# First keys and values of an attention kernel: VectorE halves two rows of each third, GpSimd adds one, and six rows are turned ahead of three

## The chip, the cores and the metric

One core of one Trainium2 chip runs the whole program. The metric is the device time of one execution in microseconds (us), inputs in the chip's memory (HBM) at the start and the output there at the end. The engines named below are TensorE (PE in the profile; PEld is its loading of weights), VectorE (DVE), ScalarE (ACT), GpSimd (POOL) and SyncE (SP), which issues most of the DMAs. Each engine runs its own queue in order and waits for the others through semaphores.

## The reference

Two parts, the second fed by the first (q and k are drawn with 0.8 times unit normal values, v with 0.1):

```python
# q, k, v: (8, 8, 576, 64); pool = 8, so Sp = 72
k_p = k.reshape(B, H, Sp, pool, D).mean(axis=3)
v_p = v.reshape(B, H, Sp, pool, D).mean(axis=3)
scores = scale * np.matmul(q, k_p.transpose(0, 1, 3, 2))
scores = scores - np.max(scores, axis=-1, keepdims=True)
attn = np.exp(scores)
attn = attn / (np.sum(attn, axis=-1, keepdims=True) + 1e-09)
attn_out = np.matmul(attn, v_p)
# x = attn_out as 4608 rows of 512; 8 experts, capacity 1152
logits = x @ w_gate
expert_idx = np.argmax(logits, axis=1)
...
h = np.maximum(np.einsum('ecd,edf->ecf', disp, w1), 0.0)   # F = 1024
y = np.einsum('ecf,efd->ecd', h, w2)
out[i] = gate_w[i] * y[expert_idx[i], pos[i]]              # rows kept by the capacity
```

The change lies in the first two lines (mean over 8 consecutive rows of k and v) and in what stands directly behind them.

## The kernel before

The function `pooled_attn_top1_moe` emits its instructions under one manual schedule: the order in which Python emits them is the order on each engine's queue. Nothing is reordered afterwards; only semaphores decide when an instruction starts.

**Pooled keys and values.** Batches go in pairs. K and V of a pair come as three thirds each, a third being a raw tile of 128 partitions x 3 rows x 512 floats (8 rows of 64 that are to be added), loaded by SP (L207) in the order k, k, k, v, v, v, with q tiles between (L223, tails L228). Seven raw buffers exist. GpSimd adds a third by halves in `tree`: 512 to 256 for each row (L370), to 128 (L372), to 64 (L374, into kp or vp). So it goes for the later pairs. For the first pair the work is split: GpSimd adds four of the nine rows (the first third and one row of the last), VectorE the other five with a reduction over the pool axis (`red`, L380).

**Turning.** TensorE transposes the pooled rows, two rows in one 128x128 transpose and the ninth alone (`turns_of`, L399 and L401), into PSUM. Copies (L406, L412) lay them out: keys into `kbs`, values into `vTp`. For the first pair ScalarE copies the even rows of batch 0, VectorE the odd and the ninth. `prep_v` then multiplies the values of a batch by the block with the expert gates (L463, TensorE) and VectorE masks the product into `vbd` (L470, L471).

**Units.** Attention is cut into 36 units of 128 query rows: four full tiles for each of two batches and one tail for both, 9 to a pair. The main loop's step n holds: the scores of unit n (L499) in two halves, its row maximum (L506) and subtraction (L511) on VectorE, the exponential of unit n-1 on ScalarE (L514), the transposes of the probabilities of unit n-2 in two parts (`p_t`: L523 on TensorE, L524 on ScalarE), the transposes of the next unit's q (L489) with ScalarE's copy qT (L490), the product with the values of unit n-2 (`av`, L535), its division (L546 to L554), and steps of the routing. Finished rows are written to `xs` from ScalarE's queue (L582). `load_kv(1)` stands ahead of the loop, `load_kv(2)` at step 5; GpSimd's trees for pair 1 are queued from step 0.

**Shared completion semaphores.** The loads of SP and the writes of xs take turns over a set of eight completion semaphores (DMAHW0 to DMAHW7 in the listings), so a DMA also waits for the one that had its semaphore last.

Behind the attention come the routing's end and the experts (from about 210 us to the end), which the change leaves as they are.

Of the kernel before, what the change touches and what calls it, by code (L numbers as in the profile page):

```python
# [21 lines left out]
P = 128  # L22
# [9 lines left out]
def pooled_attn_top1_moe(ctx: ExitStack, tc: tile.TileContext, q, k, v, wg, w1, w2, cap, out):  # L32
# [135 lines left out]
    with ExitStack() as actx:  # L168
# [207 lines left out]
                left[due] -= 1  # L376
            yield

        def red(dst, t):
            nc.vector.tensor_reduce(out=dst, in_=t.rearrange("p c (j d) -> p c d j", j=POOL), axis=AX.X, op=ALU.add)  # L380

        def pooled(p):

# [3 lines left out]
        def third(i):  # L387
            return slice(i * NR // 3, (i + 1) * NR // 3)
# [41 lines left out]
            summed("v", p)  # L430
            copies(vTp, slice(0, None), turns_of(bank([P, 4, P], "pk"), vps[p]))

        def keys_first(u, made):

            if u:
                for x in range(2):
                    copies(kbs[0][x * D : (x + 1) * D, x, u], slice(u * H + x, (u + 1) * H, 2), made)
                return
            for o, copy in ((0, nc.scalar.copy), (1, nc.vector.tensor_copy)):
                for x in range(2):  # L440
                    v, hs = kbs[0][x * D : (x + 1) * D, x, 0], slice(x, H, 2)
                    done = [even(v, hs, made, o, copy)]
                    if o:
                        done.append(last(v, hs, made, copy))
                    for d_ in done:
                        if o == 0:
                            tc.add_to_no_dep_group("first", d_.ins)
                        else:
                            tc.declare_no_dep(d_.ins, group="first", reason="other columns, other quadrants")

        def values_first(u, made):
            if u == 0:
                last(vTp, slice(0, None), made)
            for o in range(2):
                even(vTp[:, u * H : (u + 1) * H], slice(u * H, (u + 1) * H), made, o)

        def prep_v(b):

# [16 lines left out]
        class Unit:  # L475
# [16 lines left out]
            def score(self, part):  # L492
                if part == 0:
                    self.ps = psc.tile([P, HH, 256], F32, name="ps", tag="ps")
                m = P // len(self.bs)
                for h in range(part * HH // 2, (part + 1) * HH // 2):
                    for u, b in enumerate(self.bs):
                        us = slice(u * m, (u + 1) * m)
                        nc.tensor.matmul(self.ps[us, h, 0 : 2 * SP_].rearrange("p (a x) -> p a x", a=2), self.qT[:, h, us],  # L499
                                         kbs[b // 2 % 2][:, :, b % 2, h], start=True, stop=True)  # L500

            def softmax(self):

# [260 lines left out]
        with tc.manual_schedule():  # L764
            rest = setup()
            pooled(0)
            head_masks()
            gq.append(tree(kps[0][:, third(0)], raws[0][0][0]))
            gq.append(tree(kps[0][:, NR - 1 :], raws[0][0][2][:, 2:3]))
            gq.append(tree(vps[0][:, third(0)], raws[0][1][0]))  # L770
            gq.append(tree(vps[0][:, 6:7], raws[0][1][2][:, 0:1]))
            drain(gq)
            red(kps[0][:, third(1)], raws[0][0][1])
            red(kps[0][:, 6 : NR - 1], raws[0][0][2][:, 0:2])
            load_kv(1)
            pk = psc.tile([P, HH, 256], F32, name="ps", tag="ps").rearrange("p a n -> p (a n)")[:, 0:512].rearrange("p (i q) -> p i q", i=4)
            kfirst = turns_of(pk, kps[0])
            keys_first(0, kfirst)
            units[0].q_part()
            gates_in()  # L780
            red(vps[0][:, third(1)], raws[0][1][1])
            red(vps[0][:, 7:], raws[0][1][2][:, 1:])
            vfirst = []

            def ahead(b):

# [312 lines left out]
            def turns(n):  # L1099

                p, j = divmod(n, NPU)
                if n == 1:
                    prep_v(0)
                    values_first(1, vfirst[0])
                if p + 1 < B // 2:
                    if j == (6 if p == 0 else 5):
                        prep_k(p + 1)
                    if j == (8 if p == 0 else 6):
                        turn_v(p + 1)
# [10 lines left out]
            def spread(n):  # L1120

                p, j = divmod(n, NPU)
                if n == 1:
                    vfirst.append(turns_of(bank([P, 4, P], "pk"), vps[0]))
                    values_first(0, vfirst[0])
                elif values_at(n):
                    prep_v(values_at(n))

# [19 lines left out]
            for n in range(nu + 2):  # L1148
# [21 lines left out]
                    start_rows()  # L1170
                if u:
                    u.score(0)
                if p and n <= nu:
                    p.p_t(0)
                if 0 < n <= nu:
                    units[n - 1].exp()
                fed = n > NB and nx and values_at(n)
                if fed:
                    nx.q_part()
                spread(n)  # L1180
                if u:
                    u.score(1)
                    if n == 0:
                        keys_first(1, kfirst)
                    u.softmax()
                step(aq)
                if p and n <= nu:
                    p.p_t(1)
                if n == nu:
                    sums()  # L1190
                if nx and not fed:
                    nx.q_part()
                if held:
                    held.clear()
                    step(rq)
# [173 lines left out]
```

## Time and profile before

| what | us |
|---|---|
| three runs | 663.55, 661.72, 657.91 |
| median | 661.72 |
| profiled execution, its own time | 656.15 |
| span of the profiled execution | 654.5 |
| TensorE busy in the span | 607.1 (93%) |
| VectorE / GpSimd / ScalarE busy | 339.2 / 317.9 / 223.6 |
| mean granted TensorE clock | 0.979 of full speed |

How to read it: the span runs from the first to the last recorded instruction of one execution, and 1.65 us lie around it. All times in the rows are counted from the span's start. A row of the timeline gives start, duration, engine, line, operation, output <- inputs, shapes and count; in brackets stands how long the engine had been idle before it and what ended that.

### The profile page before, as it was taken

The numbers are of one execution on the slowest core, as the hardware profiler recorded it, in microseconds if no ns is written. First come the engines' busy times: TensorE is split into PE (matmuls) and PEld (weight loads), VectorE is DVE, ScalarE is ACT, GpSimd is POOL, SyncE is SP. The second block draws the span as 40 slices with busy tenths as digits, with TensorE's granted clock in tenths as the row PEclk, the third lists the DMA queues.
The fourth block names the chain that finished last, engine by engine and source line by source line (L and its number), as shares of the span: only waits on it lengthen the run. The fifth ranks groups of instructions, "written<-read, shape, count | busy, mean of one in ns | idle before, by whom it ended". The sixth has DMA issues, their size and how long they took to land. (4 is left out here: it accounts for less than half of the span.)

```text
span 654.5 us, 13915 instructions
## 1 busy us (share of the span) xinstructions
PE 607.1 (93%) x3966; PEld 539.8 (82%) x3967; DVE 339.2 (52%) x740; ACT 223.6 (34%) x414; POOL 317.9 (49%) x537
## 2 busy tenths in 40 slices
PE   2899979989779799999999999999999999999994
PEld 2789869878668588898989899888998889989983
DVE  4777867868767812246728642235432565222222
ACT  2465444546424111135517521115211473112111
POOL 7399979247645334215745413414444155431344
PEclk9999989999979899999999999999999999999997
DMA  9999996584622271107845652102721091110111
GB/s 314 301 255 334 310 264 121 118 242 98 177 46 54 73 300 64 32 32 238 298 159 178 248 204 64 64 20 77 263 64 56 12 316 31 64 42 22 64 48 65
DMA packets 103712, 93.79 MB, mean 143 GB/s; under 512 B 82820, under 2 KB 82820, under 8 KB 103688
## 3 DMA queue, kind: packets, MB, share of 16 engines
q1 hardware_dynamic: 54520, 62.47, 30.1%
q0 software_dynamic: 11392, 21.57, 10.4%
q10 hardware_dynamic: 37776, 9.46, 6.5%
q8 instruction: 12, 0.20, 0.1%
q14 instruction: 12, 0.10, 0.1%
HBM read 132.96 MB, written 31.27 MB: 251 GB/s over the span
## 5 line engine op out<-in xcount | busy, mean ns | idle before, releaser
L1269 DVE SCALAR_TENSOR_TENSOR hl<-ph,hh 128x512 fp32r<-128x512 f32 x60 | 40.8, 690 | 108.9 <-ACT hh L1268 78.0
L1268 ACT ACTIVATE hh<-ph 128x512 fp32r<-128x512 f32 x60 | 35.9, 599 | 171.2 <-PE ph L152 168.3
L165 PE MATMUL y<-w2h,hh 128*128 128x512 f32 x280 | 78.1, 400 | 0.0
L152 PE MATMUL ph<-xh,w1h 128*128 128x256 f32 x480 | 76.5, 281 | 1.2 <-ACT xo L1084 0.9
L165 PE MATMUL y<-w2l,hh 128*128 128x512 f32 x280 | 76.6, 395 | 0.0
L152 PE MATMUL ph<-xl,w1h 128*128 128x256 f32 x480 | 76.2, 280 | 0.4 <-DVE w1l L128 0.3
L152 PE MATMUL ph<-xh,w1l 128*128 128x256 f32 x480 | 76.0, 280 | 0.0
L97 POOL DMA_INDIRECT xg<-xs,ix x42 | 44.2, 1053 | 58.9 <-PE y L165 52.2
L165 PE MATMUL y<-w2h,hl 128*128 128x512 f32 x280 | 71.0, 396 | 0.0
L152 PEld LDWEIGHTS ph<-xh,w1h 128*128 128x128 f32 x480 | 65.7, 188 | 4.5 <-issue 1.9
L152 PEld LDWEIGHTS ph<-xl,w1h 128*128 128x128 f32 x480 | 65.0, 188 | 0.7 <-issue 0.7
L152 PEld LDWEIGHTS ph<-xh,w1l 128*128 128x128 f32 x480 | 65.0, 188 | 0.0
L165 PEld LDWEIGHTS y<-w2h,hl 128*128 128x128 f32 x280 | 52.6, 188 | 12.7
L165 PEld LDWEIGHTS y<-w2l,hh 128*128 128x128 f32 x280 | 52.6, 188 | 12.6
L535 PE MATMUL pa<-vbd,pT 126*128 126x146 f32 (+5 forms) x400 | 60.6, 313 | 0.0
L535 PEld LDWEIGHTS pa<-vbd,pT 126*128 126x128 f32 (+1 forms) x400 | 56.4, 184 | 3.0 <-issue 0.7
L165 PEld LDWEIGHTS y<-w2h,hh 128*128 128x128 f32 x280 | 50.0, 188 | 9.4
L524 ACT COPY pT<-pp 126x384 f32<-126x384 f32 x72 | 30.3, 422 | 78.6 <-PE pp L523 56.7
L128 DVE TENSOR_TENSOR xl<-px,xh 128x512 fp32r<-128x512 f32 x40 | 25.7, 686 | 57.2 <-ACT xh L127 57.2
L102 POOL DMA_INDIRECT out_dram<-zrow,iz x40 | 46.8, 1171 | 16.3 <-issue 15.1
L499 PE MATMUL ps<-kbs,qT 128*128 128x144 f32 (+1 forms) x320 | 52.9, 308 | 1.8 <-ACT qT L490 1.8
L95 POOL TENSOR_TENSOR guard<-ix 128x4 int32<-128x4 int32 x21 | 5.1, 244 | 101.6 <-DVE ix L92 101.3
(261 smaller groups left out, 1035.6 us busy)
## 6 DMA issues: line engine op xcount, KB each, us to landing
r<-in_moe_w_dram SPq DMA_DIRECT2D x86, 1024.0 KB
raw<-in_k_dram SPq DMA_DIRECT2D x12, 768.0 KB
raw<-in_v_dram SPq DMA_DIRECT2D x12, 768.0 KB
qblk<-in_q_dram SPq DMA_DIRECT2D x32, 256.0 KB
xs<-xo ACTq DMA_DIRECT2D x16, 512.0 KB
raw<-in_moe_w_dram SPq DMA_DIRECT2D x4, 512.0 KB
qtail<-in_q_dram SPq DMA_DIRECT2D x8, 128.0 KB
xs<-xo ACTq DMA_DIRECT2D x8, 128.0 KB
```

The costliest lines, as they stand in the source:

```text
L95: nc.gpsimd.tensor_sub(guard, ix, ix)
L97: nc.gpsimd.indirect_dma_start(out=dst[:, i, :].bitcast(F32), out_offset=None, in_=src, in_offset=bass.IndirectOffsetOnAxis(ap=ix[:, i, 0: ...
L102: ins = nc.gpsimd.indirect_dma_start(out=out[:, :], out_offset=bass.IndirectOffsetOnAxis(ap=i_, axis=0), in_=src, in_offset=None, bounds_c ...
L128: eng.tensor_sub(lo, src, hi.bitcast(F32))
L152: nc.tensor.matmul(p[:, f2], a[:, c, f * P : (f + 1) * P], b[:, c], start=(f2 == 0 and j == 0 and c == 0), stop=(f2 == 1 and j == 2 and c ...
L165: nc.tensor.matmul(y, a[:, c, i * P : (i + 1) * P], b[:, c], start=(first and n == 0), stop=(last and n == len(terms) - 1))
L499: nc.tensor.matmul(self.ps[us, h, 0 : 2 * SP_].rearrange("p (a x) -> p a x", a=2), self.qT[:, h, us], kbs[b // 2 % 2][:, :, b % 2, h], sta ...
L524: nc.scalar.copy(self.pT[:, cs.start : cs.stop], pp[0:KC, 0 : len(cs)])
L535: made = nc.tensor.matmul(self.pa[us, h0 * XW : (h0 + nh) * XW], self.pT[:, c, us], vbd[b % 2][:, c, 0:nh].rearrange("r s x -> r (s x)"), ...
L1268: nc.scalar.activation(hh[s], p, AF.Relu)
L1269: nc.vector.scalar_tensor_tensor(out=hl[s], in0=p, scalar=0.0, in1=hh[s].bitcast(F32), op0=ALU.max, op1=ALU.subtract)
```

## The change

- `red` goes. `pair_sum` takes its place on VectorE: rows 0 and 1 of a third are added by three halving adds (128x512, 128x256, 128x128 results), with scratch from the pool of the `xo` tiles. VectorE so takes six of nine rows, GpSimd the last row of each third, K's three first and then V's.
- K: six rows (three transposes, `turn_six`) are turned as soon as the first two thirds are pooled, then q of unit 0, then the last three rows (`turn_three`, two transposes). ScalarE lays out the six, VectorE and ScalarE the three.
- q of unit 1 is turned between the two halves of unit 0's scores; the keys of batch 1 are laid out behind that (`keys_one`), by ScalarE (six rows, row 8) and VectorE (rows 6 and 7).
- V: VectorE's three sums stand behind those copies, with the softmax of unit 0 between the first and the second. The six rows are turned in step 1, then the first part of unit 0's probabilities, q of unit 2, and the three rows. `prep_v(0)` moves from the end of step 1 to between the halves of unit 2's scores.

```diff
@@ -376,8 +376,14 @@

-        def red(dst, t):
-            nc.vector.tensor_reduce(out=dst, in_=t.rearrange("p c (j d) -> p c d j", j=POOL), axis=AX.X, op=ALU.add)
+        def pair_sum(dst, t):
+            sc = wk.tile([P, 2, H, XW - 1], F32, name="xo", tag="xo", bufs=3).rearrange("p i h x -> p (i h x)")
+            t1 = sc[:, 0:W].rearrange("p (i x) -> p i x", i=2)
+            t2 = sc[:, W : 3 * W // 2].rearrange("p (i x) -> p i x", i=2)
+            nc.vector.tensor_add(t1, t[:, :, 0 : W // 2], t[:, :, W // 2 :])
+            nc.vector.tensor_add(t2, t1[:, :, 0 : W // 4], t1[:, :, W // 4 :])
+            nc.vector.tensor_add(dst, t2[:, :, 0:D], t2[:, :, D:])

@@ -430,29 +436,45 @@

-        def keys_first(u, made):
...
-        def values_first(u, made):
...
+        turned = pall[:, 0 : 3 * P].rearrange("p (i q) -> p i q", i=3)
+        def turn_six(x):
+            for i in range(3):
+                nc.tensor.transpose(turned[:, i], x[:, 2 * i : 2 * i + 2].rearrange("p r d -> p (r d)"), ident)
+        def turn_three(x):
+            aside(nc.tensor.transpose(side[0:D, 0:P], x[:, 6], ident))
+            aside(nc.tensor.transpose(side[:, P : 2 * P], x[:, 7:9].rearrange("p r d -> p (r d)"), ident))
+        def laid(v, hs, src, rs, copy=nc.scalar.copy):
+            return copy(v.rearrange("d h (g r) -> d h g r", r=NR)[:, :, :, rs], src.rearrange("d i (h g) -> d h g i", g=GP)[:, hs])
+        def six(v, hs):
             for o in range(2):
-                even(vTp[:, u * H : (u + 1) * H], slice(u * H, (u + 1) * H), made, o)
+                laid(v, hs, turned[o * D : (o + 1) * D], slice(o, 6, 2))
+        def three(v, hs, copy=nc.scalar.copy):
+            made = [laid(v, hs, side[D:, P : 2 * P].rearrange("d (i q) -> d i q", i=1), slice(8, 9)),
+                    laid(v, hs, side[0:D, 0 : 2 * P].rearrange("d (i q) -> d i q", i=2), slice(6, 8), copy)]
+            for d_ in made:
+                aside(d_)
+            return made
+        def keys_of(u):
+            return [(kbs[0][x * D : (x + 1) * D, x, u], slice(u * H + x, (u + 1) * H, 2)) for x in range(2)]
+        def keys_six(u):
+            for v, hs in keys_of(u):
+                six(v, hs)
+        def keys_three(u):
+            for v, hs in keys_of(u):
+                a, b = three(v, hs, nc.vector.tensor_copy)
+                tc.add_to_no_dep_group("first", a.ins)
+                tc.declare_no_dep(b.ins, group="first", reason="other columns, other quadrants")
+        def values_of(u):
+            return vTp[:, u * H : (u + 1) * H], slice(u * H, (u + 1) * H)

@@ -496,8 +518,10 @@
                         us = slice(u * m, (u + 1) * m)
-                        nc.tensor.matmul(self.ps[us, h, 0 : 2 * SP_].rearrange("p (a x) -> p a x", a=2), self.qT[:, h, us],
+                        made = nc.tensor.matmul(self.ps[us, h, 0 : 2 * SP_].rearrange("p (a x) -> p a x", a=2), self.qT[:, h, us],
                                          kbs[b // 2 % 2][:, :, b % 2, h], start=True, stop=True)
+                        if self is units[0]:
+                            tc.add_to_no_dep_group("scores", made.ins)

@@ -765,22 +789,37 @@
             head_masks()
-            gq.append(tree(kps[0][:, third(0)], raws[0][0][0]))
-            gq.append(tree(kps[0][:, NR - 1 :], raws[0][0][2][:, 2:3]))
-            gq.append(tree(vps[0][:, third(0)], raws[0][1][0]))
-            gq.append(tree(vps[0][:, 6:7], raws[0][1][2][:, 0:1]))
+            for kv in range(2):
+                for i in range(3):
+                    gq.append(tree((kps, vps)[kv][0][:, 3 * i + 2 : 3 * i + 3], raws[0][kv][i][:, 2:3]))
             drain(gq)
-            red(kps[0][:, third(1)], raws[0][0][1])
-            red(kps[0][:, 6 : NR - 1], raws[0][0][2][:, 0:2])
+            def pairs_of(dst, kv, i):
+                pair_sum(dst[:, 3 * i : 3 * i + 2], raws[0][kv][i][:, 0:2])
+            for i in range(3):
+                pairs_of(kps[0], 0, i)
             load_kv(1)
-            pk = psc.tile([P, HH, 256], F32, name="ps", tag="ps").rearrange("p a n -> p (a n)")[:, 0:512].rearrange("p (i q) -> p i q", i=4)
-            kfirst = turns_of(pk, kps[0])
-            keys_first(0, kfirst)
+            turn_six(kps[0])
+            keys_six(0)
             units[0].q_part()
-            gates_in()
-            red(vps[0][:, third(1)], raws[0][1][1])
-            red(vps[0][:, 7:], raws[0][1][2][:, 1:])
-            vfirst = []
+            turn_three(kps[0])
+            keys_three(0)
+            def keys_one():
+                for v_, hs in keys_of(1):
+                    for o in range(2):
+                        other(laid(v_, hs, turned[o * D : (o + 1) * D], slice(o, 6, 2)))
+                for v_, hs in keys_of(1):
+                    a, b = three(v_, hs, nc.vector.tensor_copy)
+                    other(a)
+                    other(b)
+                    tc.add_to_no_dep_group("first", a.ins)
+                    tc.declare_no_dep(b.ins, group="first", reason="other columns, other quadrants")
+            def other(made):
+                tc.declare_no_dep(made.ins, group="scores", reason="the other batch's columns")

@@ -1099,9 +1138,6 @@
                 p, j = divmod(n, NPU)
-                if n == 1:
-                    prep_v(0)
-                    values_first(1, vfirst[0])
                 if p + 1 < B // 2:
@@ -1120,9 +1156,8 @@
                 p, j = divmod(n, NPU)
-                if n == 1:
-                    vfirst.append(turns_of(bank([P, 4, P], "pk"), vps[0]))
-                    values_first(0, vfirst[0])
+                if n == 2:
+                    prep_v(0)
                 elif values_at(n):
@@ -1170,26 +1205,42 @@
                     u.score(0)
-                if p and n <= nu:
+                if p and 2 < n <= nu:
                     p.p_t(0)
                 if 0 < n <= nu:
                     units[n - 1].exp()
                 fed = n > NB and nx and values_at(n)
                 if fed:
                     nx.q_part()
+                if n == 0:
+                    nx.q_part()
                 spread(n)
                 if u:
                     u.score(1)
                     if n == 0:
-                        keys_first(1, kfirst)
+                        keys_one()
+                        pairs_of(vps[0], 1, 0)
                     u.softmax()
+                if n == 0:
+                    gates_in()
+                    for i in range(1, 3):
+                        pairs_of(vps[0], 1, i)
+                if n == 1:
+                    turn_six(vps[0])
+                    six(*values_of(0))
+                    units[0].p_t(0)
                 step(aq)
                 if p and n <= nu:
                     p.p_t(1)
                 if n == nu:
                     sums()
-                if nx and not fed:
+                if nx and n and not fed:
                     nx.q_part()
+                if n == 1:
+                    turn_three(vps[0])
+                    for v_, hs in (values_of(0), values_of(1)):
+                        three(v_, hs)
+                    six(*values_of(1))
                 if held:
```

VectorE's queue, from the first pooled keys to unit 1's softmax (kp and vp are the pooled rows, kbs the laid-out keys, mx and pt the softmax, xo in the new adds a scratch tile). Before:

```order
L380 TENSOR_REDUCE kp<-raw 128x128 [waits DMAHW3_49]
L412 COPY kbs_143<-ps 64x32x4 [waits PE_49]
L406 COPY kbs_143<-pa 64x32
L412 COPY kbs_143<-ps 64x32x4
L406 COPY kbs_143<-pa 64x32
L380 TENSOR_REDUCE vp<-raw 128x192 [waits DMAHW7_49]
L380 TENSOR_REDUCE vp<-raw 128x128 [waits DMAHW0_49]
L506 TENSOR_REDUCE mx<-ps 128x8 [waits PE_49]
L511 TENSOR_TENSOR pt<-ps,mx 128x576 [waits DVE_49]
L506 TENSOR_REDUCE mx<-ps 128x8 [waits PE_49]
```

With the change:

```order
L386 TENSOR_TENSOR kp<-xo 128x128 [waits DVE_49]
L450 COPY kbs_143<-pa 64x32x2 [waits PE_49,Activation_49]
L450 COPY kbs_143<-pa 64x32x2
L450 COPY kbs_143<-pa 64x32x2 [waits Activation_49]
L450 COPY kbs_143<-pa 64x32x2
L384 TENSOR_TENSOR xo<-raw 128x512 [waits DMAHW5_49]
L385 TENSOR_TENSOR xo<-xo 128x256 [waits DVE_49]
L386 TENSOR_TENSOR vp<-xo 128x128 [waits DVE_49]
L530 TENSOR_REDUCE mx<-ps 128x8 [waits PE_49]
L535 TENSOR_TENSOR pt<-ps,mx 128x576 [waits DVE_49]
L384 TENSOR_TENSOR xo<-raw 128x512 [waits DMAHW7_49]
L385 TENSOR_TENSOR xo<-xo 128x256 [waits DVE_49]
```

The third copy into kbs now waits for a ScalarE instruction (its four copies of batch 1), and all sums of V and unit 0's softmax stand behind it; two of V's three sums stand behind that softmax. ScalarE's queue in the same place (identr-turned q becomes qT, wgi is the block with the gates), before:

```order
L412 COPY kbs_143<-ps 64x32x4 [waits PE_49]
L412 COPY kbs_143<-ps 64x32x4
L490 COPY qT<-pq 128x512 [waits PE_49]
L270 COPY wgi<-wgt 64x16 [waits DMAHW0_49]
L271 COPY wgi<-wgt 64x4x16
L272 COPY wgi<-wgt 64x3x8 [waits Activation_49]
L273 COPY wgi<-wgt 64x2x8
L406 COPY kbs_143<-pa 64x32 [waits DVE_49]
```

With the change:

```order
L450 COPY kbs_143<-pa 64x32x3 [waits PE_49]
L450 COPY kbs_143<-pa 64x32x3 x3
L512 COPY qT<-pq 128x512 [waits PE_49]
L450 COPY kbs_143<-pa 64x32 [waits PE_49]
L450 COPY kbs_143<-pa 64x32 [waits DVE_49]
L512 COPY qT<-pq 128x512 [waits PE_49]
L450 COPY kbs_143<-pa 64x32x3 [waits DVE_49]
L450 COPY kbs_143<-pa 64x32x3 x3
```

The copies of batch 1 (the last two rows) stand behind the second qT. TensorE's queue from V's transposes to the first product with the values, before:

```order
L401 MATMUL pk<-identr,vp 128x128 [waits Pool_49]
L499 MATMUL ps<-kbs_143,qT 128x144 x2
L489 MATMUL pq<-identr,qblk 128x128 [waits DMAHW1_49,PE_49]
L489 MATMUL pq<-identr,qblk 128x128 x3
L463 MATMUL pa<-wgi,vTp 126x80 [waits Activation_49]
L463 MATMUL pa<-wgi,vTp 126x88 x2
L463 MATMUL pa<-wgi,vTp 126x80 x2
L499 MATMUL ps<-kbs_143,qT 128x144 [waits DVE_49,Activation_49]
```

With the change:

```order
L443 MATMUL pa<-identr,vp 128x128 [waits Pool_49]
L547 MATMUL pp<-identr,pt 126x128 [waits PE_49,Activation_49]
L547 MATMUL pp<-identr,pt 126x128 x2
L511 MATMUL pq<-identr,qblk 128x128 [waits DMAHW1_49,PE_49]
L511 MATMUL pq<-identr,qblk 128x128 x3
L446 MATMUL pa<-identr,vp 64x128 [waits DVE_49,Activation_49]
L447 MATMUL pa<-identr,vp 128x128 [waits Pool_49]
L521 MATMUL ps<-kbs_143,qT 128x144 [waits Activation_49]
L521 MATMUL ps<-kbs_143,qT 128x144
L485 MATMUL pa<-wgi,vTp 126x80 [waits Activation_49]
```

`prep_v(0)` (L463, now L485) stands behind the first half of unit 2's scores and waits for the last of the eight copies into vTp, of both batches, where before it waited for the third of five.

## Rows read from the trace of the kernel before

**Rows 1.** The page of the profile: its first line, and its first part (busy us, share of the span and instructions of each engine).

```profile
span 654.5 us, 13915 instructions
...
PE 607.1 (93%) x3966; PEld 539.8 (82%) x3967; DVE 339.2 (52%) x740; ACT 223.6 (34%) x414; POOL 317.9 (49%) x537
```

**Rows 2.** Busy time of PE, PEld, DVE, ACT and POOL in stretches (each with its count), then the granted TensorE clock, the DMA share and GB/s.

```profile
8.00:22.00 14.00, 7.97 (x32) 6.65 (x33) 11.38 (x10) 3.63 (x14) 8.22 (x13) 1.00 1.17 301
...
48.00:50.00 2.00, 2.00 (x17) 1.93 (x15) 1.50 (x3) 1.41 (x4) 1.92 (x4) 1.00 0.19 43
96.00:100.00 4.00, 4.00 (x18) 3.76 (x18) 1.45 (x5) 0.58 (x1) 3.73 (x7) 0.50 1.19 235
```

**Rows 3.** The timeline from 5 to 15 us, the first K: the adds and reductions, the first q and the first scores.

```profile
5.80 2.08 POOL L370 TENSOR_TENSOR t<-raw 128x256 f32<-128x256 f32 x3 [1.05 <-DMA raw<-in_k_dram]
...
7.83 4.56 DVE L380 TENSOR_REDUCE kp<-raw 128x192 f32<-128x1536 f32 x2 [5.57 <-DMA raw<-in_k_dram]
...
9.90 0.73 POOL L370 TENSOR_TENSOR t<-raw 128x256 f32<-128x256 f32 x1 [0.28 <-DMA raw<-in_k_dram]
...
10.71 0.46 POOL L372 TENSOR_TENSOR t<-t 128x128 f32<-128x128 f32 x1
11.24 0.32 POOL L374 TENSOR_TENSOR kp<-t 128x64 f32<-128x64 f32 x1
...
12.71 1.06 PE L489 MATMUL pq<-identr,qblk 128*128 128x128 f32 x4
...
14.45 2.29 PE L499 MATMUL ps<-kbs,qT 128*128 128x144 f32 x8 [0.68 <-ACT qT L490]
```

**Rows 4.** The timeline from 15 to 29 us, the first V: VectorE's reductions, GpSimd's last add, unit 0's softmax, V's transposes, q, `prep_v`, the masked values and the first product with the values.

```profile
15.98 4.61 DVE L380 TENSOR_REDUCE vp<-raw 128x192 f32<-128x1536 f32 x2 [1.98 <-DMA raw<-in_v_dram]
...
18.08 0.73 POOL L370 TENSOR_TENSOR t<-raw 128x256 f32<-128x256 f32 x1 [1.19 <-DMA raw<-in_v_dram]
...
19.41 0.32 POOL L374 TENSOR_TENSOR vp<-t 128x64 f32<-128x64 f32 x1
20.49 0.77 DVE L506 TENSOR_REDUCE mx<-ps 128x8 f32<-128x576 f32 x1
...
20.87 1.06 PE L401 MATMUL pk<-identr,vp 128*128 128x128 f32 x4
21.30 0.76 DVE L511 TENSOR_TENSOR pt<-ps,mx 128x576 f32<-128x576 f32 x1
...
22.61 0.60 PE L489 MATMUL pq<-identr,qblk 128*128 128x128 f32 x4
...
23.77 1.32 PE L463 MATMUL pa<-wgi,vTp 64*126 64x80 f32 x10 [0.57 <-ACT vTp L412]
...
25.24 0.24 DVE L470 TENSOR_TENSOR vbd<-pa,mk 126x80 f32<-126x80 f32 x1 [0.88 <-PE pa L463]
...
26.21 0.28 DVE L471 TENSOR_TENSOR vbd<-pa,mk 126x128 f32<-126x128 f32 x1
...
27.17 1.58 PE L535 MATMUL pa<-vbd,pT 126*128 126x146 f32 x10
```

**Rows 5.** Groups of instructions by line, shapes kept apart (busy us, mean ns of one | idle before); the window is 0 to 30 us, for the L1061 row the whole span.

```profile
L490 ACT COPY qT<-pq 128x512 f32<-128x512 f32 x4 | 2.3, 586 | 0.3 <-PE pq L489 0.3
...
L412 ACT COPY kbs<-ps 64x128 f32<-64x128 f32 x6 | 1.7, 284 | 9.2 <-PE ps L401 7.5 <-PE ps L499 1.7
L412 ACT COPY vTp<-pk 64x256 f32<-64x256 f32 x4 | 1.7, 423 | 0.0
...
L524 ACT COPY pT<-pp 126x384 f32<-126x384 f32 x2 | 1.0, 478 | 2.7 <-PE pp L523 2.7
...
L406 DVE COPY kbs<-pa 64x32 f32<-64x32 f32 x2 | 0.4, 209 | 0.0
...
L1061 DVE TENSOR_TENSOR w2l<-r,w2h 128x512 fp32r<-128x512 f32 x4 | 2.5, 673 | 0.0
```

**Rows 6.** The timeline at 90 and at 126 us: one VectorE instruction of the routing with two inputs in SBUF, beside an add of GpSimd and alone.

```profile
89.95 0.99 POOL L372 TENSOR_TENSOR t<-t 128x384 f32<-128x384 f32 x1
90.03 0.94 DVE L684 SCALAR_TENSOR_TENSOR gix<-ghi,gci 128x9 int32<-128x9 f32 x1
...
126.12 0.16 DVE L684 SCALAR_TENSOR_TENSOR gix<-ghi,gci 128x9 int32<-128x9 f32 x1
```

**Rows 7.** The timeline: GpSimd's first add of pair 1's K, the load of pair 2's K, and the end of pair 1's V with its first transpose.

```profile
28.60 0.73 POOL L370 TENSOR_TENSOR t<-raw 128x256 f32<-128x256 f32 x1 [8.87 <-DMA raw<-in_k_dram]
...
44.72 0.37 ACTq L582 DMA_DIRECT2D xs<-xo  x1
...
49.63 1.38 SPq L207 DMA_DIRECT2D raw<-in_k_dram  x3
...
50.85 0.59 POOL L374 TENSOR_TENSOR vp<-t 128x192 f32<-128x192 f32 x1
...
52.13 0.27 PE L399 MATMUL pa<-identr,vp 128*64 128x128 f32 x1
```

**Rows 8.** Waits of SP's DMA queue over the whole span (us in total, times, longest us).

```profile
SPq L207 <- DMA xs<-xo: 22.0, 5, 12.4
```

**Rows 9.** The timeline from 95 to 98.5 us, the first work of TensorE behind its longest wait of the attention.

```profile
95.07 1.09 PE L489 MATMUL pq<-identr,qblk 128*128 128x128 f32 x4 [3.73 <-DMA qblk<-in_q_dram]
...
96.09 2.41 PE L463 MATMUL pa<-wgi,vTp 64*126 64x80 f32 x10
```

More of the change, by code (lines that the diff above doesn't have):

```diff
@@ L431, in turn_v @@
             copies(vTp, slice(0, None), turns_of(bank([P, 4, P], "pk"), vps[p]))
-        def keys_first(u, made):
[L435 to L449, printed above, removed]
@@ L451, in values_first @@
-        def values_first(u, made):
-            if u == 0:
-                last(vTp, slice(0, None), made)
-            for o in range(2):
-                even(vTp[:, u * H : (u + 1) * H], slice(u * H, (u + 1) * H), made, o)
+        turned = pall[:, 0 : 3 * P].rearrange("p (i q) -> p i q", i=3)
[5 more added lines that the diff above has]
+            aside(nc.tensor.transpose(side[:, P : 2 * P], x[:, 7:9].rearrange("p r d -> p (r d)"), ident))
```

## The prediction

> **What bounds the kernel now.** I read the page first: TensorE is busy 93% of a span of 654.5 us [rows 1]. That is an average; the change acts only in the first 30 us, so I then read the timeline there. In 8 to 22 us TensorE is busy 7.97 of 14.00 us and VectorE 11.38 [rows 2]: TensorE waits for pooled rows, and the first 27 us are a chain. It runs over K: the thirds start to be added at 5.80, 7.83 and 9.90, as they land; VectorE's two reductions end at 7.83 + 4.56 = 12.39; then transposes, copies and qT, first scores at 14.45 [rows 3]. Then over V: `prep_v` at 23.77, the masked values from 25.24 to 26.49, the first product with the values at 27.17 [rows 4]. From there TensorE has work for a long while. So the change is worth what it does to that 27.17, unless something later gives it back. What the reader should look for in these rows is who stands last before the first scores and before `prep_v`.
>
> **K's sums.** Removed: the reductions, 4.56 us for five rows. Added: three sums of two rows each. One takes three adds: 0.673 for 128x512 [rows 5], 0.28 for the 128x128 (from another 128x128 product of VectorE at 26.21 [rows 4]), and 0.41 between them for the 128x256, an estimate on the line through the two; 1.36 together, 1.45 with the gaps. GpSimd's row takes 9.90 to 11.56 = 1.66 with gaps, 1.51 without (0.73 + 0.46 + 0.32) [rows 3]. How the two run beside each other is the first unknown. Side by side, K is ready at 11.56, when GpSimd's row of the third that lands at 9.90 ends. Strictly in turn, a third costs 1.36 + 1.51 = 2.87, three end at 5.80 + 8.61 = 14.41. The nearest row: a VectorE operation with two inputs in SBUF took 0.94 us beside a GpSimd add and 0.16 alone, and ended 0.03 us behind that add [rows 6]; it is nearer to taking turns. I take 2.45 a third (turns, with a little overlap at each handover), so K is ready at 13.15: 0.8 later than before.
>
> [...]
>
> **First scores.** Six rows and q are turned before K's last third is there, which is what the new order gains: behind the sums only two transposes and the copies remain, about 1.05 (half of four transposes, 1.06 / 2 [rows 3], and two copies of 0.21 to 0.28 [rows 5]). First scores 14.2, against 14.45.
>
> **The second q amid the scores, and its tail.** Half of unit 0's scores takes 2.29 / 2 = 1.15, q's four transposes 1.06 [rows 3], qT 0.59 [rows 5]: 14.2 + 2.8 = 17.0. ScalarE then lays out batch 1 with four copies of 0.28 [rows 5]: 18.15. VectorE stands with its third copy into kbs until the last of these is done (the listing shows that wait), then does two of 0.21 [rows 5]: 18.55. Queued behind that waiting instruction are all of V's sums and unit 0's softmax. Before, VectorE began on V at 15.98 [rows 4].
>
> **V.** First sum 1.45, and 0.6 more because GpSimd's last V row lies there (18.08 to 19.73 before [rows 4]): 20.6. Softmax of unit 0, 0.77 + 0.76 [rows 4]: 22.2. Second sum 23.65, third 25.1. Before, its part of V ended at 15.98 + 4.61 = 20.59 [rows 4], ahead of the softmax.
>
> **To prep_v.** From the second sum: three transposes 0.8 (of 1.06 for four): 24.45; two copies of 0.4: 25.25 (0.423 for one of 256 elements where these have 192 [rows 5]); the probabilities' copy 0.48 and qT 0.59 [rows 5]: 26.3; four copies of the three last rows, 0.95 (two at 0.2 and two at 0.28, as of kbs above): 27.3; two of 0.4: 28.1. `prep_v` waits for the last of them, so it starts at 28.15 against 23.77. That it may now start later in its step doesn't matter, the copies are what it waits for.
>
> **To the first product.** `prep_v` 1.32 and the masked values 26.49 - 25.24 = 1.25 [rows 4], with handovers 2.7: 30.85 against 27.17. **Loss: 3.7 us.** Its bounds: with adds side by side K is 1.6 and V's first sum 0.6 earlier, +1.4; strictly in turn K is 1.25 later, which takes V's sum out of GpSimd's way (-0.6), +4.3.
>
> **Whether it is given back.** GpSimd's adds for pair 1 wait for their loads (8.87 us, to 28.60) and end at 51.44, 0.7 before TensorE needs them at 52.13 [rows 7]: they aren't late, so nothing is won or lost there. The load of pair 2's K left SP at 49.63 [rows 7], and SP's longest waits for this load end with a write of xs [rows 8], the nearest one issued at 44.72 [rows 7], while the DMA share was 0.19 in 48 to 50 us [rows 2]. Writes of xs are finished units, so later units make later loads, and TensorE's long wait for a q tile, 3.73 us to 95.07 [rows 9], moves along. I give nothing back. The scratch for the adds comes from the pool of the xo tiles, first written by units behind 28 us: no cost. SP's queue keeps its order.
>
> **The sum.** 656.15 (the profiled execution's own time: 654.5 and 1.65 around) + 3.7 = 659.85. The median of the runs shown, 661.72, lies 5.57 above this execution; on it the forecast is 665.4, own range 663.1 (+1.4) to 666.0 (+4.3).
>
> **Rivals.**
> - *Strict turns*: the adds of both engines never overlap, +4.3: 666.0. For it: 0.94 beside, 0.16 alone [rows 6]. Against: the two chains also have gaps that the other can use. [...]
> - [...] TensorE now stands more between 17 and 28 us. If `prep_v` and the first product come at half pace: 2.41 - 1.32 = 1.09, 1.58 x 0.83 = 1.3, and some 0.6 for scores between: 3.0 on top, 668.4. Against: in 8 to 22 us the granted clock reads 1.00 with TensorE busy only 57% [rows 2].
> - *The other side, lost start absorbed*: if the loads behind the q tile of 95.07 are paced by the DMAs and not by the units, TensorE arrives 3.7 later at a tile that lands when it did, the wait of 3.73 goes, and with it the half pace behind it: (1.09 - 0.60) + (2.41 - 1.32) + half of the 1.5 us left to 100, 2.3 us. It decides at whether that tile lands by 95.1: 656.15 - 2.3 = 653.85, on the median 659.4. Against: the pause in the DMAs at 48 to 50 [rows 2], which the xs write set.
> - *The chain isn't late*: ScalarE's copies run early enough that V's sums start as before, and nothing changes: 661.7. Against: the order of both queues.
>
> **Chances.** Forecast 0.43; strict turns 0.12; half pace 0.20; absorbed 0.15; not late 0.10. The three runs lie 5.6 us apart, so 1% (6.6 us) is about what tells a difference from none. 8 in 10 need all but the tails: from 659.0, just below the absorbed case, to 669.3, half pace with the scatter of a median. Faster by 1% means below 655.1, out of reach but for scatter: 0.02. Slower by 1%, above 668.3, is half of the half-pace case and a little of the others: 0.12. Within 1%: 0.86.
>
> **What would show it.** K's last add on VectorE at about 13.2 (11.6: side by side; 14.4: strict turns), VectorE's 128x512 add at well over 0.67 beside GpSimd; first scores at about 14.2; VectorE idle before its third copy into kbs, released by ScalarE, with V's first sum at 18.5; `prep_v` at 28, released by a copy into vTp, the first product at 31, and the same lag at the load of pair 2's K and at the q tile of 95.07. The prediction is wrong if the lag at the first product is under 1.4 or above 4.3, if `prep_v` takes well over 1.32, or if the lag is gone after 100 us.

## The result, and the profile after it

The changed kernel's median is 666.43 us (664.19 to 667.94, 7 runs), that of the kernel before 661.72 us (657.91 to 663.55, 7 runs); the ratio is 1.0093, 95% interval 1.0072 to 1.0115. That is slower beyond the noise, by about 1% (the interval reaches a little past it). 665.4 was forecast, with a range of 659.0 to 669.3.

The profiled execution took 666.43, the median itself, while the one of before lay 5.57 below the median of its kernel. So the two profiles are 10.2 us apart where the medians are 4.7 apart: the profiles tell where time goes, the medians how much.

The page after, its first line and first part (as [rows 1]):

```profile
span 664.7 us, 13942 instructions
...
PE 616.6 (93%) x3966; PEld 548.5 (83%) x3967; DVE 338.5 (51%) x754; ACT 225.7 (34%) x421; POOL 321.5 (48%) x539
```

The timeline after, from 5 to 34 us: what stands here answers to [rows 3] and [rows 4]. L384 to L386 are VectorE's adds, L370 to L374 GpSimd's, L450 the copies, L521 the scores, L485 `prep_v`, L559 the product with the values.

```profile
5.46 0.69 DVE L384 TENSOR_TENSOR xo<-raw 128x512 f32<-128x512 f32 x1 [3.20 <-DMA raw<-in_k_dram]
5.51 1.22 POOL L370 TENSOR_TENSOR t<-raw 128x256 f32<-128x256 f32 x1 [0.76 <-DMA raw<-in_k_dram]
6.19 0.83 DVE L385 TENSOR_TENSOR xo<-xo 128x256 f32<-128x256 f32 x1
...
11.35 0.43 DVE L386 TENSOR_TENSOR kp<-xo 128x128 f32<-128x128 f32 x1
...
11.71 0.32 POOL L374 TENSOR_TENSOR kp<-t 128x64 f32<-128x64 f32 x1
...
13.29 1.30 PE L521 MATMUL ps<-kbs,qT 128*128 128x144 f32 x4 [0.73 <-DVE kbs L450]
...
17.12 0.48 DVE L450 COPY kbs<-pa 64x64 f32<-64x64 f32 x2 [3.98 <-ACT kbs L450]
...
17.64 0.69 DVE L384 TENSOR_TENSOR xo<-raw 128x512 f32<-128x512 f32 x1
...
21.75 0.42 DVE L385 TENSOR_TENSOR xo<-xo 128x256 f32<-128x256 f32 x1
...
22.21 0.29 DVE L386 TENSOR_TENSOR vp<-xo 128x128 f32<-128x128 f32 x1
...
27.31 2.42 PE L485 MATMUL pa<-wgi,vTp 64*126 64x80 f32 x10 [0.51 <-ACT vTp L450]
...
32.05 1.89 PE L559 MATMUL pa<-vbd,pT 126*128 126x146 f32 x10
```

K is pooled at 12.03 (before: 12.39), and the first scores start 1.16 earlier than before. Then VectorE stands 3.98 us in front of its third copy into kbs, released by ScalarE, and V's first sum starts at 17.64. `prep_v` starts 3.54 later than before and takes 2.42 instead of 1.32; the first product comes at 32.05 instead of 27.17, 4.88 later.

The stretches after (columns as in [rows 2]): the granted clock, 1.00 from 8 to 22 us, reads 0.61 in 22 to 24 and 0.50 from 24 to 32, behind a stretch in which TensorE was busy 0.11 of 2 us.

```profile
20.00:22.00 2.00, 0.11 (x1) 0.00 (x0) 1.93 (x4) 0.68 (x1) 0.00 (x0) 1.00 1.33 207
22.00:24.00 2.00, 1.35 (x7) 1.39 (x8) 1.90 (x6) 0.64 (x2) 0.00 (x0) 0.61 1.30 219
...
28.00:30.00 2.00, 2.00 (x10) 1.86 (x10) 0.14 (x1) 0.00 (x0) 1.81 (x3) 0.50 1.03 421
```

The loads of pair 3's V and the long wait for a q tile (timelines of SP's queue, ScalarE's and TensorE; [rows 9] answer to the last):

```profile
91.70 0.81 SPq L207 DMA_DIRECT2D raw<-in_v_dram  x2
...
79.52 0.37 ACTq L606 DMA_DIRECT2D xs<-xo  x1
...
101.87 1.09 PE L511 MATMUL pq<-identr,qblk 128*128 128x128 f32 x4 [5.99 <-DMA qblk<-in_q_dram]
```

Two thirds of V leave only when a write of xs has landed, and TensorE waits 5.99 us for the q tile instead of 3.73. The tile came 6.80 later: 4.5 by which the units lag there, and 2.3 us more. Why two thirds wait, where one did before, stands in the compiled programs. The building of the program gave the DMAs' completion semaphores out otherwise once the engines' work had changed, though SP's own order is the same: pair 3's fifth third (V's second) now has the semaphore that a write of xs had last, before it had one of a q tail. In the kernel before only the sixth third stood behind a write of xs. By these semaphores the write in question is the one issued at 79.52, and not the next one at 89.82. SP's queue stood 12.1 us for it, because the write itself was slow to land: in 80 to 88 us ScalarE's DMA queue moved 0.13 MB while SP's moved 2.95, and in 88 to 92 us, with SP's earlier loads through, 0.67. In before the write of 74.31 held the sixth third until 87.40 in the same way.

### The profile page after: what moved, and what is told of

The parts are those of the page before. It is cut to its first block, busy times and chain, and to the rows that moved or that the text cites. A ratio compares the mean times of both kernels' runs of the same rounds, so it can differ in the third digit from the quotient of the medians.

```text
span 664.7 us, 13942 instructions
## 1 busy us (share of the span) xinstructions
PE 616.6 (93%) x3966; PEld 548.5 (83%) x3967; DVE 338.5 (51%) x754; ACT 225.7 (34%) x421; POOL 321.5 (48%) x539
## 5 line engine op out<-in xcount | busy, mean ns | idle before, releaser
L559 PE MATMUL pa<-vbd,pT 126*128 126x146 f32 (+5 forms) x400 | 63.4, 321 | 0.1
L559 PEld LDWEIGHTS pa<-vbd,pT 126*128 126x128 f32 (+1 forms) x400 | 58.8, 191 | 3.3 <-ACT kbs L412 0.7
L521 PE MATMUL ps<-kbs,qT 128*128 128x144 f32 (+1 forms) x320 | 55.4, 318 | 1.1 <-DVE kbs L450 0.7
```

The costliest lines, as they stand in the source:

```text
L521: made = nc.tensor.matmul(self.ps[us, h, 0 : 2 * SP_].rearrange("p (a x) -> p a x", a=2), self.qT[:, h, us], kbs[b // 2 % 2][:, :, b % 2, ...
L559: made = nc.tensor.matmul(self.pa[us, h0 * XW : (h0 + nh) * XW], self.pT[:, c, us], vbd[b % 2][:, c, 0:nh].rearrange("r s x -> r (s x)"), ...
```

## The experiments

They ran on three other chips of the same kind, where the kernel before takes 646.5, 648.6 and 648.5 us: the first four on the first, the next four (the change repeated, the two with freed semaphores, the first run with the shorter list) on the second, the last three on the third. Each ratio is to runs of the kernel before on the same chip, beside it; start times of different chips, each from one profiled execution, are to be compared to some tenths only. "First product" is the start of TensorE's first product with the values, "q wait" the longest wait for a q tile near 100 us.

**The kernel before, once more.** No edit.

> The kernel before once more, to see how far two profiled executions of one program lie apart. If the start sets the time, its first product with the values comes at 27.2 again, and the wait for the q tile at 91 to 95 us (3.7 us) is there again. If the profile shown of before was a lucky execution (656.15 against a median of 661.7), the q tile's wait is longer, nearer to the 6.0 us of the changed kernel, with the start unchanged. Ratio to before 1.000 within 0.3%.

Ratio 1.0013 (0.9982 to 1.0044). First product 26.75, q wait 4.65 (3.73 in the profile shown of before): between the two values expected. Two executions of the same program, on two chips, differ in the wait by almost 1 us.

**Reductions again, in the new order.** The cause could be the adds beside GpSimd.

```diff
 def pair_sum(dst, t):
...
-    nc.vector.tensor_add(t1, t[:, :, 0 : W // 2], t[:, :, W // 2 :])
-    nc.vector.tensor_add(t2, t1[:, :, 0 : W // 4], t1[:, :, W // 4 :])
-    nc.vector.tensor_add(dst, t2[:, :, 0:D], t2[:, :, D:])
+    nc.vector.tensor_reduce(out=dst, in_=t.rearrange("p c (j d) -> p c d j", j=POOL), axis=AX.X, op=ALU.add)
```

> The changed kernel with one part undone: VectorE adds its two rows of each third with one reduction instead of three halving adds; rows, order and turning stay as changed. Theory (the order makes the loss, and the adds beside GpSimd cost only some tenths): K's last sum ends at 11.5 instead of 12.0, since GpSimd's adds are then not blocked, V's second sum ends within 0.4 of 22.5, prep_v at 27.3 within 0.5, ratio to before still 1.006 to 1.011. Rival (the contention of the adds makes the loss): prep_v comes 2 us or more earlier and the ratio falls to 1.000 to 1.004.

Its timeline: a reduction of two rows takes 1.89, and GpSimd's add beside it 0.73 instead of 1.22.

```profile
5.32 1.89 DVE L381 TENSOR_REDUCE kp<-raw 128x128 f32<-128x1024 f32 x1 [3.06 <-DMA raw<-in_k_dram]
5.37 0.73 POOL L370 TENSOR_TENSOR t<-raw 128x256 f32<-128x256 f32 x1 [0.61 <-DMA raw<-in_k_dram]
```

K's last sum ends at 11.46 and V's second at about 22.5, as expected. First scores 12.96, 0.45 earlier than in the change's repeat below (13.41), of which 0.31 is that the first third of K was there earlier (5.32, 5.63). `prep_v` at 27.25, first product 32.00, q wait 5.83; ratio 1.0125 (1.0088 to 1.0162). The adds are not what costs: without them the loss is the same.

**V's sums ahead of the copies that wait.**

```diff
             keys_three(0)
+            for i in range(2):
+                pairs_of(vps[0], 1, i)
...
                         keys_one()
-                        pairs_of(vps[0], 1, 0)
                     u.softmax()
                 if n == 0:
                     gates_in()
-                    for i in range(1, 3):
+                    for i in range(2, 3):
```

> The changed kernel with VectorE's first two sums of V moved ahead of its copies of batch 1's keys, so that they no longer stand behind the copy that waits for ScalarE. Theory (that wait delays V): V's second sum ends at about 18 instead of 22.5, prep_v starts at 24 to 25 instead of 27.3, the first product at 27 to 28 instead of 32.05, ratio to before 0.998 to 1.005. Rival (the adds beside GpSimd, or ScalarE's longer list of copies, delay prep_v): prep_v at 26.5 to 27.3 and the ratio at 1.007 to 1.011.

VectorE's queue in its timeline, V's second sum and the copies behind it, and TensorE's `prep_v`:

```profile
15.78 0.69 DVE L384 TENSOR_TENSOR xo<-raw 128x512 f32<-128x512 f32 x1 [0.60 <-DMA raw<-in_v_dram]
16.50 0.83 DVE L385 TENSOR_TENSOR xo<-xo 128x256 f32<-128x256 f32 x1
17.37 0.43 DVE L386 TENSOR_TENSOR vp<-xo 128x128 f32<-128x128 f32 x1
17.73 0.47 DVE L450 COPY kbs<-pa 64x64 f32<-64x64 f32 x2
...
24.21 1.32 PE L485 MATMUL pa<-wgi,vTp 64*126 64x80 f32 x10 [1.08 <-ACT vTp L450]
```

V's second sum ends at 17.80 instead of 22.50, `prep_v` starts at 24.21 and runs at full pace, the first product comes at 27.78: all as the theory had it. Ratio 1.0048 (1.0017 to 1.0079): better than the change by 0.0057 (against its repeat below, on the second chip; the two other runs in the changed order on this chip gave 1.0125 and 1.0103), some 3.7 us, and still above 1. Its q wait is 6.25.

**TensorE given work in the gap.** Twelve more transposes of the identity, written over by V's.

```diff
                 if n == 1:
+                    for i in range(12):
+                        nc.tensor.transpose(turned[:, i % 3], ident, ident)
                     turn_six(vps[0])
```

> The changed kernel with twelve more transposes of the identity on TensorE, written over later, in the gap before V's transposes (18.9 to 22.6 us, where it waits). Theory (TensorE falls to its lower clock at about 26 us because it stood still): granted clock 1.00 in 20 to 30 instead of 0.62, prep_v takes 1.3 to 1.5 instead of 2.42, the first product comes 1.0 to 1.8 earlier, and the ratio to before falls by 0.001 to 0.003. Rival (the lower clock comes from something else, or the later waits take the gain back): prep_v at 2.4 again, or an earlier first product with the end unchanged.

```profile
18.93 1.81 PE L1230 MATMUL pa<-identr 128*128 128x128 f32 x12
...
27.58 1.32 PE L485 MATMUL pa<-wgi,vTp 64*126 64x80 f32 x10 [0.76 <-ACT vTp L450]
```

The twelve took 1.81 us and filled about half of the gap: TensorE then still stood 2.11 us until V's second sum was there. `prep_v` took 1.32 as before, and the first product came at 30.35 (32.16 in the change's repeat). The forecast of a granted clock of 1.00 missed: 22 to 26 us show 0.63, 26 to 30 show 0.95, so it fell and rose again ahead of `prep_v`. So the run shows what `prep_v` at full pace is worth here, and not that standing still is what lowers the clock. Ratio 1.0103 (1.0066 to 1.0139), not to be told from the change's: 1.8 us at the start are within the interval, so whether the end keeps them stays open. Its q wait is 6.03.

**The change, repeated on the second chip.** No edit.

> The changed kernel again, on the chip of the experiments. Theory: two losses. The start (first product at 32.0 against 26.8 for the kernel before on this chip), and in pair 3's V two thirds instead of one wait for a write of xs, because the completion semaphores fell differently to the DMAs: the wait for the q tile at about 96 us is 5.8 to 6.2 instead of 4.65. Ratio to before 1.006 to 1.012. Rival: the longer wait was chance, and it is at 4.7 or less here.

Ratio 1.0105 (1.0066 to 1.0143), first product 32.16, `prep_v` 2.41 long, q wait 6.32. The longer q wait was no chance.

**The semaphores freed, in the change and in the kernel before.** Two tiny loads in the change, three in the kernel before.

```diff
             def hooks(n):
                 p, j = divmod(n, NPU)
+                if n == 12:
+                    for _ in range(2):
+                        nc.sync.dma_start(sm.tile([1, 64], F32, name="tiny", tag="tiny", bufs=3), q[0, 0, 0:1, :])
```

> The changed kernel with two loads of 256 bytes put on SP at step 12, ahead of pair 3's K and V; they fill a tile that nothing reads, and move the completion semaphores on, so that none of pair 3's six thirds shares one with a late write of xs. Theory (sharing makes the q tile late): the start is as changed (first product at 32.0), all six thirds leave by 84 us instead of 92.5, the wait for the q tile falls from about 6.0 to 1 to 3.5, and the ratio to before falls to 1.000 to 1.006. Rival (the q tile is late because the units are late): the wait stays at 5.5 to 6.2 and the ratio at 1.006 to 1.012.

> The kernel before with three loads of 256 bytes on SP at step 12, as in the run with the freed semaphores: none of pair 3's thirds then shares one with a late write of xs (before: one). Theory (sharing makes the q tile late): start unchanged (first product at 26.8), wait for the q tile 1 to 3 instead of 4.65, ratio to before 0.993 to 0.998. Rival: wait at 4.5 or more, ratio 0.999 to 1.002.

Both missed. All six thirds left early (by 81.4 and 78.6 us), but TensorE stood twice, 2.52 and then 4.55 for the q tile in the change, 2.28 and 4.24 in the kernel before, and the ratios are 1.0109 (1.0059 to 1.0160) and 1.0048 (1.0015 to 1.0080). The sharing had only moved: in the freed change, a write of xs on ScalarE's queue itself waited for an earlier write of xs that had its semaphore, and with it the copies behind it (timeline of ScalarE):

```profile
95.95 0.37 ACTq L606 DMA_DIRECT2D xs<-xo  x1
96.42 0.48 ACT L548 COPY pT<-pp 126x384 f32<-126x384 f32 x1 [3.50 <-DMA xs<-xo]
```

In the kernel before so edited, moreover, TensorE's granted clock fell to 0.50 at the start, where nothing had been edited: its stretches show it, and `prep_v` took 2.42, the first product came at 29.71.

```profile
22.00:24.00 2.00, 1.20 (x6) 0.80 (x5) 1.26 (x2) 1.96 (x6) 0.00 (x0) 0.50 1.35 216
24.00:30.00 6.00, 6.00 (x28) 5.83 (x28) 2.54 (x6) 2.07 (x5) 1.76 (x3) 0.50 1.09 365
```

**V's sums ahead, and a shorter list on ScalarE.**

```diff
                 if n == 1:
                     turn_six(vps[0])
                     six(*values_of(0))
+                    units[0].exp()
                     units[0].p_t(0)
...
-                        three(v_, hs)
-                    six(*values_of(1))
+                        three(v_, hs, nc.vector.tensor_copy)
...
                 if n == 2:
                     prep_v(0)
+                    six(*values_of(1))
```

This is on top of the edit before; the exponential of unit 0 goes from its old place.

> The changed kernel with V's first two sums ahead of VectorE's copies of batch 1's keys, and ScalarE's list to prep_v shortened: six rows of batch 0's values ahead of unit 0's exponential, rows 6 and 7 of the values copied by VectorE, six rows of batch 1 behind prep_v(0). Its listing has one third of pair 3's V sharing a semaphore with a late write of xs, as before the change. Theory (queue order at the start, and the sharing): prep_v at 22.7 to 23.7, first product 25.7 to 26.8, wait for the q tile 4.0 to 5.0, ratio to before 0.996 to 1.002. Rival (the adds, or what the start wins is waited away at pair 1's V, which is ready only 0.7 ahead of its use): first product 26.8 or later, or an earlier one with ratio 1.002 to 1.008.

> The kernel with V's sums ahead and ScalarE's shorter list once more, beside the two others. Theory: first product 26.8 to 27.8, wait for the q tile 3.7 to 4.7, ratio 0.996 to 1.002: the loss of the change is undone, and nothing is won over the kernel before. Rival (the earlier result was chance): ratio 1.003 to 1.008.

The timeline of its first run:

```profile
23.64 1.32 PE L485 MATMUL pa<-wgi,vTp 64*126 64x80 f32 x10 [0.49 <-DVE vTp L450]
27.25 1.68 PE L559 MATMUL pa<-vbd,pT 126*128 126x146 f32 x10 [0.94 <-ACT vTp L450]
```

`prep_v` at 23.64 and 23.50, first product 27.25 and 27.10 (25.7 to 26.8 was expected of the first, and missed: it stands 0.94 for the six rows of batch 1 that were put behind `prep_v`), q wait 3.92 and 3.71, ratio 0.9995 (0.9963 to 1.0027) and 0.9980 (0.9953 to 1.0007). With the adds, the split of rows and the six-before-three turning all kept, the loss is gone. Nothing is won over the kernel before that the intervals could show. One third waits for a write of xs here, not two; the last run below tells whether that is what undid the loss.

**Two thirds made to wait.** One tiny load in the kernel before, two in the last kernel, placed as above; each gives pair 3's fifth third the semaphore of a write of xs.

> The kernel before with one load of 256 bytes on SP at step 12 (into a tile that nothing reads). It shifts the completion semaphores so that pair 3's fifth third shares with a late write of xs, and two thirds wait for it, as in the changed kernel; nothing is changed at the start. Theory (the sharing makes the q tile late): first product at 26.8 (or 29.7, if TensorE falls to its lower clock at the start, as it did once), the fourth third of pair 3's load group leaves at about 74 and the fifth after 85, the wait for the q tile is 5.6 to 6.4 instead of 3.7 to 4.7, ratio to before 1.002 to 1.006. Rival (the longer wait follows from the late start): wait 3.7 to 4.7, ratio 0.998 to 1.002.

> The kernel with V's sums ahead and ScalarE's shorter list, and two loads of 256 bytes on SP at step 12, which make two thirds of pair 3 wait for the write of xs instead of one. Theory (sharing): start as without them (first product 26.8 to 27.8), wait for the q tile 5.6 to 6.4 instead of 3.9, ratio 0.002 to 0.006 above that of the same kernel without the two loads. Rival: wait 3.7 to 4.7 and the two ratios equal within 0.001.

The kernel before, repeated (first three lines) and with one tiny load (the others), in the timelines of SP, ScalarE and TensorE; the write of xs is the one whose semaphore the waiting third has:

```profile
73.92 0.41 ACTq L582 DMA_DIRECT2D xs<-xo  x1
87.28 0.33 SPq L207 DMA_DIRECT2D raw<-in_v_dram  x1
95.50 1.09 PE L489 MATMUL pq<-identr,qblk 128*128 128x128 f32 x4 [4.65 <-DMA qblk<-in_q_dram]
```

```profile
76.28 0.37 ACTq L582 DMA_DIRECT2D xs<-xo  x1
88.28 1.54 SPq L207 DMA_DIRECT2D raw<-in_v_dram  x2
99.30 1.09 PE L489 MATMUL pq<-identr,qblk 128*128 128x128 f32 x4 [6.08 <-DMA qblk<-in_q_dram]
```

Two thirds wait instead of one, and the q wait is 6.08; in the other kernel 5.78. Over all executions, one waiting third gives 3.71 to 4.65 (four, with the first product at 26.75 to 27.25), two give 5.78 to 6.32 (seven, with the first product anywhere from 27.40 to 32.16). The last kernel parts the two causes: its first product came at 27.40 (27.25 and 27.10 without the loads) and TensorE reached the wait 0.8 later, while the wait itself grew by 1.9 to 2.1. The kernel before with one tiny load doesn't, since `prep_v` took 2.42 at its start and the first product came at 29.18. The ratios are 1.0022 (0.9994 to 1.0051) and 0.9991 (0.9965 to 1.0018; 0.0011 above the same kernel without the loads, though the execution profiled, 655.79, lay 7.3 above its median): expected were 0.002 to 0.006 in both, and only the first is within, barely. So the sharing lengthens this wait by some 2 us, which is shown, but its price in the whole is about 1 us and not to be told from none. With two thirds waiting as in the change, and the start mended, the time is not to be told from that of the kernel before: so it is the start that carries the loss, as far as the intervals tell. The 1.0048 of V's sums ahead is more than its first product's lag of 1.0 us (0.0016) accounts for, but its interval begins at 1.0017, so nothing has to be left over.

## Why the prediction was right

The time fell into the range, and the main wait was the one forecast. But two of the signs that the prediction itself named for being wrong came: the lag at the first product was 4.88, above 4.3, and `prep_v` took 2.42, well over 1.32. The third did not: the lag was there after 100 us, 6.80 at the q tile and 8.4 at the next write of xs (112.83 instead of 104.40). So the path was right in its first half, and how near the forecast came to the time is in part luck.

**The step that carried it.** VectorE's third copy into kbs waits for ScalarE's last copy of batch 1, and V's sums and the softmax stand behind it: forecast, found (3.98 us, released by ScalarE), and undone by moving V's sums (V's second sum 4.7 earlier, 0.0057 of the time) and by ScalarE's shorter list (ratio back to 0.9980 to 0.9995). At `prep_v` the sums are worth 3.2 us (27.42 in the change's repeat, 24.21), the list of eight copies between V's sums and `prep_v` 0.6 to 0.7 (23.64, 23.50). That the list's step took as much from the whole time as the sums' (0.0053 and 0.0068, each to some 0.004) is hard to square with 0.7 us, and no run shows where the rest comes from.

**K's sums** were mis-sized: 2.45 a third were taken, and K was to be ready at 13.15. It was ready at 12.03: the thirds were added from 5.46, 7.64 and 9.62, 2.3 to 2.4 each with GpSimd's part, and 0.34 of the difference is that the first began at 5.46 and not 5.80. VectorE's first add of a third took 0.69 in the first two thirds, where it began just ahead of GpSimd's, as alone (0.68), and 0.83 in the last, where GpSimd's add was under way. Its second took 0.83 instead of 0.42 and its third 0.43 instead of 0.29, GpSimd's first 1.22 instead of 0.73. So they hinder each other, by some 0.5 at most for an instruction, and strict turns (14.4) are out. With reductions in their place GpSimd's add took 0.73, so it is the halving adds that make it longer. Nor did the add that began second wait for all of the other: GpSimd's first add ran beside 0.64 us of VectorE's and was 0.49 longer, and a third took 2.3 to 2.4 where strict turns give 2.87.

**The rest of the chain** ran about 0.9 ahead of the forecast: first scores 13.29 (14.2), V's first sum from 17.64 (18.55), second sum ended at 22.50 (23.65), `prep_v` 27.31 (28.15). `prep_v` so came 3.54 late instead of 4.4.

**Half pace** was a rival at 0.20, and came. Its numbers are those of `prep_v` behind the long q wait, 2.41 [rows 9] against 1.32 at the start [rows 4], at a granted clock of 0.50 [rows 2]. In all four executions profiled with the changed order and no added work in the gap `prep_v` took 2.41 or 2.42 (the change twice, with reductions, with freed semaphores). It gave 1.10 at `prep_v`. From `prep_v` to the first product the forecast took 2.7; it was 4.74, and 2.77 in the run with twelve more transposes, where `prep_v` ran at full pace. So half pace cost 2.0 there, and the first product was 4.88 late instead of 3.7. That the median still fell near 665.4 rests on two errors of opposite sign at the start, 0.9 too late in the chain and 2.0 for the half pace left out: that is luck.

**"SP's queue keeps its order"** was true and not enough. The order stayed, the semaphores that the DMAs share did not, and a second third fell behind a write of xs. The forecast's sentence that the waits for loads move along with the units (the xs writes of 74.31 and 85.04 come at 79.52 and 89.82, pair 2's K at 55.04 instead of 49.63 [rows 7]) held; the q wait grew on top of it, so it was the opposite of the rival in which the lost start is absorbed there.

**The size.** Forecast were +3.7 on the median; measured +4.7 by the medians, 0.0093 by the runs' ratio, which is 6 us, and 666.43 lies 0.4 above the forecast's own range. Three terms are found: the late chain, the half pace and the longer q wait. Their single prices can't be added up to the total from these runs: the half pace is some 2 us at the start, the q wait 2 us there and about 1 in the whole, and an interval is 0.003, 2 us, wide to either side.

## What to carry to other kernels

When work is moved on an in-order queue, read what then stands behind each waiting instruction: the change won 1.16 us for the first scores and lost 3.5 at the next stage, most of it because one copy that waited was put ahead of independent sums. An edit on one engine can give the DMAs other completion semaphores; after a change, compare which DMA each load waits for, not its place in the queue only. And put work that is ready where the engine would have stood anyway: the sums of V had 3.98 us of idle VectorE in front of them, and with two of them put there `prep_v` came 3.2 us earlier (24.21, 27.42).

## What the runs showed of the hardware that was not expected

- Whether `prep_v` runs at half pace is not fixed by the instructions around it. Four executions have the kernel before's start, instruction for instruction: `prep_v` took 1.32 in two and 2.42 in two (the two with tiny loads at step 12, which come far behind it), and the first product came at 27.17 and 26.75, or 29.71 and 29.18. Each of the four ran on another chip, and what decided between them is not shown.
- The granted clock's column doesn't tell all of it: in the kernel before with one tiny load it reads 1.00 in 22 to 24 us and in 24 to 30 us, where `prep_v` took 2.42 from 23.35 (1.32 from 23.35 in the kernel before, repeated); the stretch has its columns as in [rows 2].

```profile
23.35 2.42 PE L463 MATMUL pa<-wgi,vTp 64*126 64x80 f32 x10
...
24.00:30.00 6.00, 6.00 (x32) 5.84 (x32) 2.60 (x7) 2.64 (x6) 1.70 (x3) 1.00 1.10 373
```

- A DMA's completion semaphore can hold up the engine that issues the next DMA on it: with the semaphores freed for SP, ScalarE stood 3.50 us behind a write of xs.
- A write that ScalarE's queue issues while SP's queue has loads under way can take long to land: the write of xs issued at 79.52 held the fifth third until 91.70, with 0.13 MB moved for ScalarE's queue in 80 to 88 us and 2.95 MB for SP's.
